# Four heads by 256 queries per attention unit, with the state-space and projection matmuls spread over the attention periods

## The chip, the cores and the metric

The kernel runs on one core of one Trainium2 chip. The metric is device microseconds (us) of one execution; lower is better.

The engines, as the profile names them: PE does matmuls and PEld is its weight load, which overlaps PE; ACT does the exponentials; DVE and POOL are two vector engines; SP issues most DMAs. "Granted clock" or PEclk is the share of full TensorE clock that the throttle granted. Two words for this kernel: PE writes its products to banks of PSUM (`ps` and `f_ps` in the views), and an "evacuation" is the copy that empties a bank into SBUF, where the other on-chip arrays lie.

## The reference, cut to what matters

```python
x = A_x                                                  # [1, 2048, 1024], bf16
g = sigmoid((x * gate_w).sum(-1, keepdims=True))
# a: diagonal complex state space model (SSM), 1024 states
Lam_bar = exp(dt * Lam);  B_bar = ((Lam_bar - 1) / Lam)[:, None] * Bmat
Bu = einsum("bld,pd->blp", x, B_bar)
for t in range(2048): h = Lam_bar * h + Bu[:, t]         # a scan over time
a = 2 * einsum("blp,dp->bld", hs, Cmat).real + x * Dskip
# b: attention, 32 heads of 32
q, k, v = x @ wqkv, split and transposed
b = softmax(q k^T * 32**-0.5) v, heads joined, @ wo
return g * a + (1 - g) * b
```

Attention needs 32 x 2048 x 2048 exponentials. Both kernels do them in 1024 ACT instructions of 128x1024 elements. The score array is held transposed (keys on the partitions), so that the exponentials can be the stationary operand ("weights") of the product with V (PV), which has only 33 columns: 32 of V and a column of ones for the softmax sum.

## The kernel before

Work is issued to the five engines in program order by a small scheduler that puts in the waits. The attention loop takes two heads and 512 queries per unit. Heads are 32 wide but Q and K are padded to 64 rows (POOL writes the masked copies), so the array is row-tiled two ways.

```python
def e_round(b):                       # one exp per round
    ...
    for h in range(2):                # L573: scores, two row tiles, 64 rows x 512 columns
        m = e.matmul(ps[:, 2*s+h, :], Ka[64*h:64*h+64, p%4, 128*kt:128*(kt+1)],
                     Qa[64*h:64*h+64, p%4, 512*qb:512*(qb+1)], ..., tile_position=(64*h, 0))
    S.op("act", lambda e: e.activation(pt[:, psl], ps[:, 2*s:2*s+2, :], ACT.Exp, scale=SCALE), ...)  # L577
    def pv(e):                        # L587: 8 pairs of weight load and 128x33 matmul
        for h in range(2):
            for qt in range(4):
                m = e.matmul(ps[:, 6, 33*gi:33*(gi+1)], pt[:, psl, h, 128*qt:128*(qt+1)], Va[...], ...)
```

The main loop fills PE between the exponentials with pieces of the next group's projections, two matmuls of 128x512 every second round, until they run out. Everything else of the SSM and the output projection comes after attention:

```python
while n < total_steps or pvq or misc or deferred:
    if n % 128 == 0: misc.extend(proj_pieces(g_next))    # last group: SSM input matmuls instead
    ...
    e_round(b)
    if n % 2 == 0: ...pop the PV tasks of earlier rounds...
    if n % 2 == 1 and misc: misc.pop(0)()                # dense filler, while there is any
    ...
    if n % 2 == 0 and bgp: bgp.pop(0)()                  # POOL: rotation tables, then fold of C
# after the loop: the rest of the SSM (u matmuls, scans, C matmuls) and the output projection
```

"Rotation tables" are built once per state block; they turn the complex scan into two real ones. "Folding C" multiplies the output matrix by complex constants, 96 elementwise operations of 128x512. Before, POOL does both during attention.

## Time and profile before

The median is 1334.15 us (2 runs, 1333.7 to 1334.61). The profiled execution spans 1338.0 us.

| stretch of the trace | us | what runs |
|---|---|---|
| to the first exp | 54.9 | loads, projection of all of group 0 |
| first to last exp | 1003.5 | attention with projections as filler |
| after the last exp | 279.6 | SSM and output projection, PE 93% busy (all the time from 1100 to 1300 us) |

These are lines of the profile page before: busy time and instructions of each engine; busy tenths in 40 equal slices of the span; the chain of waits that ended last, as shares of the span; and four of the costliest groups (line, engine, operation, output and input, count; then busy us, mean ns of one; then idle us of the engine just before them and what ended most of it).

```profile
PE 1225.9 (92%) x13313; PEld 592.2 (44%) x13313; DVE 346.0 (26%) x784; ACT 1039.1 (78%) x1218; POOL 330.6 (25%) x662
...
PE   4699989989998998999899989989988599999997
...
ACT  0399999999999999999999999999988522332211
...
PEclk8789969978995998699789959977998799999999
...
ACT 57%; PE 36%; DVE 3%; DMA 3%; issue 1%; SPq 0%; POOL 0%; POOLq 0%
...
L577 ACT ACTIVATE arena<-ps 128x1024 bf16<-128x1024 f32 x1024 | 952.7, 1039 | 32.9 <-PE ps L573 19.7
L587 PE MATMUL ps<-arena 128*128 128x33 bf16 x8192 | 373.6, 182 | 69.8 <-ACT arena L577 58.5
L573 PE MATMUL ps<-arena 64*128 64x512 bf16 x2048 | 424.1, 432 | 0.0
L587 PEld LDWEIGHTS ps<-arena 128*128 128x128 bf16 x8192 | 278.3, 98 | 288.6 <-ACT arena L577 151.2
```

PE is 92% busy over the whole span, but the chain is ACT for most of it and PE for the end: the kernel has two phases with two limits. In the last eight slices PE reads 9 (7 in the last) and ACT 1 to 3: a tail with no exponentials.

The windows view before, for the exps alone. The columns are the stretch, its length, ACT busy time in exps and their count, granted clock, DMA share, and GB/s.

```profile
80.00:170.00 90.00, 89.96 (x99) 0.99 0.02 5
170.00:192.00 22.00, 19.67 (x22) 0.50 0.01 1
192.00:285.00 93.00, 93.00 (x102) 1.00 0.17 38
285.00:312.00 27.00, 24.81 (x26) 0.50 0.00 1
```

While filler lasts, ACT is busy all the time and an exp comes every 0.92 us. Where it has run out (170 to 192 us, 285 to 312 us) the clock is granted at 0.50 and ACT has gaps. A window counts instructions that cross its edge in both neighbours, so counts are about one too high.

The timeline before, in a stretch with filler: start us, duration, then the instructions.

```profile
86.86 0.39 PE L573 MATMUL ps<-arena 64*128 64x512 bf16 x2
87.18 0.62 PEld L587 LDWEIGHTS ps<-arena 128*128 128x128 bf16 x16 [0.23 <-issue]
...
87.83 0.39 PE L573 MATMUL ps<-arena 64*128 64x512 bf16 x2
```

From the start of the scores to that of PV is 0.32 us, and from PV to the next scores 0.65 us. How that 0.65 divides into work and waiting becomes important below (the views merge the sixteen pairs into one line).

### The profile page before, as it was taken

To read this page: it belongs to the slowest core of one execution; us is meant where nothing else is said; L and a number is where in the kernel's file an instruction comes from. 1 tells how busy PE (TensorE), PEld (TensorE's weight loads), DVE (VectorE), ACT (ScalarE), POOL (GpSimd) and SP (SyncE) were. 2 spreads that over 40 slices of the span, in tenths; PEclk is the share of its full clock that TensorE was granted. 3 is DMA by queue.
4 is the path that set the end of the run, shared out by engine and by line. 5 is a ranking of instruction groups with operands and counts; after the bars stand their busy time and mean duration, and the time that the engine had idled before them with its cause. 6 is when DMAs were issued, how large, how long until landed. Compare 5 with 4: busy or idle time off the path is not lost.

```text
span 1338.0 us, 29670 instructions
## 1 busy us (share of the span) xinstructions
PE 1225.9 (92%) x13313; PEld 592.2 (44%) x13313; DVE 346.0 (26%) x784; ACT 1039.1 (78%) x1218; POOL 330.6 (25%) x662
## 2 busy tenths in 40 slices
PE   4699989989998998999899989989988599999997
PEld 1344634544463455345444534543433244444443
DVE  0211101100110110011001101100157668888840
ACT  0399999999999999999999999999988522332211
POOL 2213324322422341344557543100000000000000
PEclk8789969978995998699789959977998799999999
DMA  7220013003100400100010000000000031111011
GB/s 149 56 41 1 2 33 72 2 1 70 35 2 2 95 10 1 39 19 2 1 41 2 1 17 2 2 1 17 2 1 1 26 85 32 32 28 29 25 48 34
DMA packets 117353, 35.57 MB, mean 27 GB/s; under 512 B 114144, under 2 KB 114144, under 8 KB 117216
## 3 DMA queue, kind: packets, MB, share of 16 engines
q1 hardware_dynamic: 117216, 33.57, 11.1%
q8 instruction: 106, 1.74, 0.5%
q14 instruction: 31, 0.25, 0.1%
HBM read 8.40 MB, written 8.39 MB: 13 GB/s over the span
## 4 chain that ended last, share of the span: by engine, by line
ACT 57%; PE 36%; DVE 3%; DMA 3%; issue 1%; SPq 0%; POOL 0%; POOLq 0%
ACT arena L577 55%; PE ps L922 8%; PE ps L573 7%; PE ps L834 6%; PE ps L587 5%; PE ps L928 4%; PE ps L809 2%; PE ps L453 2%; DMA xT<-in_A_x_dram 2%; DVE arena L859 1%; DMA arena<-in_B_wo_dram 1%; PE ps L925 1%; PE ps L485 0%; DVE arena L399 0%; ACT L577 0%
## 5 line engine op out<-in xcount | busy, mean ns | idle before, releaser
L577 ACT ACTIVATE arena<-ps 128x1024 bf16<-128x1024 f32 x1024 | 952.7, 1039 | 32.9 <-PE ps L573 19.7
L587 PE MATMUL ps<-arena 128*128 128x33 bf16 x8192 | 373.6, 182 | 69.8 <-ACT arena L577 58.5
L573 PE MATMUL ps<-arena 64*128 64x512 bf16 x2048 | 424.1, 432 | 0.0
L587 PEld LDWEIGHTS ps<-arena 128*128 128x128 bf16 x8192 | 278.3, 98 | 288.6 <-ACT arena L577 151.2
L399 DVE CAST arena<-ps 128x512 bf16<-128x512 f32 x96 | 66.5, 693 | 508.7 <-PE ps L453 348.4
L453 PE MATMUL ps<-xT,arena 128*128 128x512 bf16 x512 | 165.5, 417 | 20.7 <-DMA arena<-in_B_wqkv_dram 10.2
L573 PEld LDWEIGHTS ps<-arena 64*128 64x128 bf16 x2048 | 91.2, 95 | 160.6 <-issue 130.5
L612 POOL TENSOR_TENSOR arena<-arena,gcol 128x8 f32<-128x8 f32 x64 | 13.0, 204 | 439.4 <-DVE arena L607 439.0
L922 PE MATMUL ps<-cT_re,arena 128*128 128x512 bf16 x256 | 98.0, 383 | 2.0 <-DMA arena<-out_dram 2.0
L922 PE MATMUL ps<-cT_im,arena 128*128 128x512 bf16 x256 | 98.0, 383 | 0.0
L607 DVE RECIPROCAL arena<-ps 128x8 f32<-128x8 f32 x64 | 13.3, 207 | 302.8 <-PE ps L587 302.8
L932 ACT ACTIVATE arena<-ps,gcol 128x512 bf16<-128x512 f32 x32 | 21.1, 679 | 79.7 <-PE ps L928 79.7
L485 PE MATMUL ps<-arena,xT 128*128 128x128 bf16 x1024 | 78.2, 221 | 3.2 <-DVE arena L399 3.2
L471 POOL TENSOR_SCALAR arena<-arena 128x512 bf16<-128x512 bf16 x64 | 48.7, 768 | 131.2 <-DVE arena L399 131.2
L859 DVE TENSOR_TENSOR_SCAN arena<-pf,init,arena 128x512 bf16<-128x512 f32 x64 | 78.5, 1269 | 0.0
L468 POOL TENSOR_SCALAR arena<-arena 128x512 bf16<-128x512 bf16 x64 | 43.7, 695 | 130.9 <-DVE arena L399 130.9
L453 PEld LDWEIGHTS ps<-xT,arena 128*128 128x128 bf16 x512 | 33.1, 101 | 91.0 <-issue 69.4
L485 PEld LDWEIGHTS ps<-arena,xT 128*128 128x128 bf16 x1024 | 57.8, 98 | 30.6 <-issue 26.0
L872 ACT ACTIVATE pf<-pf 128x1 f32<-128x1 f32 x24 | 7.1, 294 | 81.6 <-DVE pf L868 81.6
L838 ACT ACTIVATE arena<-ps 128x512 bf16<-128x512 f32 x48 | 27.6, 592 | 44.3 <-PE ps L834 44.3
L928 PE MATMUL ps<-arena 128*128 128x512 bf16 x256 | 60.5, 379 | 0.0
L834 PE MATMUL ps<-xT,bT_re 128*128 128x512 bf16 x192 | 47.0, 389 | 3.0 <-issue 3.0
(124 smaller groups left out, 738.9 us busy)
## 6 DMA issues: line engine op xcount, KB each, us to landing
arena<-in_B_wqkv_dram SPq DMA_DIRECT2D x24, 256.0 KB, 4.1
out_dram<-arena SPq DMA_DIRECT2D x8, 512.0 KB, 3.8
out_dram<-arena SPq DMA_DIRECT2D x16, 256.0 KB, 2.0
arena<-in_B_wo_dram SPq DMA_DIRECT2D x1, 2048.0 KB, 8.6
arena<-out_dram SPq DMA_TRANSPOSE x16, 3.1
bT_re<-in_A_B_re_dram SPq DMA_TRANSPOSE x8, 3.1
bT_im<-in_A_B_im_dram SPq DMA_TRANSPOSE x8, 3.1
cT_re<-in_A_C_re_dram SPq DMA_TRANSPOSE x8, 3.1
```

Source lines behind the costliest of these rows:

```text
L399: S.op("dve", lambda e: e.tensor_copy(dst, src), reads=r, writes=w, name=name)
L453: m = e.matmul(ps[:, 7, :], wring[:, g % 2, qk, dt_, :], xT[:, dt_, 512 * ch:512 * (ch + 1)], start=(dt_ == 0), stop=(dt_ == 7))
L468: pool(lambda e, dst=dst, mcol=mcol: e.tensor_scalar(dst, nat[:, 0, nb, :], mcol, 0.0, ALU.mult, ALU.add), [("nat", 0, nb), "msk"], [("qa" ...
L471: pool(lambda e, dst=dst, mcol=mcol, ocol=ocol: e.tensor_scalar(dst, nat[:, 1, nb, :], mcol, ocol, ALU.mult, ALU.add), [("nat", 1, nb), "m ...
L485: m = e.matmul(ps[:, 7, 128 * qtr:128 * (qtr + 1)], xT[:, dt_, 128 * kt:128 * (kt + 1)], wring[:, g % 2, 2, dt_, :], start=(dt_ == 0), sto ...
L573: m = e.matmul(ps[:, 2 * s + h, :], Ka[64 * h:64 * h + 64, p % 4, 128 * kt:128 * (kt + 1)], Qa[64 * h:64 * h + 64, p % 4, 512 * qb:512 * ( ...
L577: S.op("act", lambda e: e.activation(pt[:, psl], ps[:, 2 * s:2 * s + 2, :], ACT.Exp, scale=SCALE), reads=[("bank", 2 * s), ("bank", 2 * s ...
L587: m = e.matmul(ps[:, 6, 33 * gi:33 * (gi + 1)], pt[:, psl, h, 128 * qt:128 * (qt + 1)], Va[:, g % 2, kt, hh, :], start=(kt == 0 and h == 0 ...
L834: m = e.matmul(ps[:, 2 * st + ri, :], bT[ri][:, dt_, 128 * j:128 * (j + 1)], xT[:, dt_, 512 * ch:512 * (ch + 1)], start=(dt_ == 0), stop=( ...
L859: dve(lambda e, ri=ri: e.tensor_tensor_scan(ht[:, ri, :], rr, ut[:, ri, :], c.init[:, ri, j:j + 1], ALU.mult, ALU.add), [("ut", ri), ("ini ...
L922: m = e.matmul(ps[:, bank, :], hpv[ri][:, j, tcols], cT[ri][:, j, 512 * cb:512 * (cb + 1)], start=first, stop=last)
L928: m = e.matmul(ps[:, bank, :], OTt[:, osl, j, :], wo[:, j, 512 * cb:512 * (cb + 1)], start=first, stop=last)
```

## The change

The intent is one pipeline for everything. Each period issues one burst of scores for four heads and 256 queries (four row tiles of 32 rows, no padding), two exps, PV of an earlier burst, and four 128x512 matmuls of "dense" work from one list: projections, gate, SSM, output projection. SSM evacuations and rotation tables are on DVE; all dense chains share one PSUM bank. The input x is loaded in smaller pieces and transposing DMAs are no longer serialized against the others. The old code stays as a fallback that a range check on the softmax sums would start.

The diff rewrites the fast path, so only its core is shown; long argument lists are cut with "...".

```diff
@@ scheduler: transposing DMAs are serialized only on request
-    def __init__(self, n_dma_lanes=12, pool_in_order=False):
+    def __init__(self, n_dma_lanes=12, pool_in_order=False, serial_xpose=False):
...
-        if dma:
+        if dma and self.serial_xpose:
@@ the attention burst (new class)
+    def burst(self, B):
+        ...
+            for kl in range(2):
+                for h in range(4):              # L1413
+                    m = e.matmul(ps[:, 2*sl[h//2]+h%2, 256*kl:256*(kl+1)],
+                                 K[32*h:32*h+32, g%2, 128*kt:128*(kt+1)],
+                                 Q[32*h:32*h+32, qz, qo:qo+256], ..., tile_position=(32*h, 0))
+        for z in range(2):                      # L1419
+            self.act(lambda e, s=s, p=p: e.activation(pt[:, p], ps[:, 2*s:2*s+2, :], ACT.Exp, scale=SCALE), ...)
@@ a dense chain: matmuls into bank 7, then one evacuation on DVE
+    def d_u(self, j, ch, n, ri):
+        ...                                     # 8 matmuls of 128x512, L1318
+        def evac():
+            self.dve(lambda e: e.tensor_copy(self.ub[:, n%2, ri, :], ps[:, 7, :]), ...)     # L1322
+            if ri == 1:
+                if ch == 0:
+                    self.bg += self.table_ops(j)       # 22 DVE operations: a rotation table
+                self.bg += self.item_ops(j, ch, n)     # 14 or 15 DVE operations: rotate, scan, rotate
@@ folding C, still on POOL
+    def pool_fold(self):
+        for j in range(8):
+            self.ld_c(j)
+            for hf in range(2):                 # 6 POOL operations of 128x512, 96 in all
+                pool(... X, ci, a2 ...); pool(... Y, cr, a2 ...); pool(... Z, cr, a1 ...)
+                pool(... cr = Z + X ...); pool(... Z, ci, b2 ...); pool(... ci = Y + Z ...)
@@ the loop over 512 periods
+        for p in range(NBURST + 2):
+            self.burst(p)
+            if p >= 2: self.pv(p - 2)
+            if p == 12 and not folded:
+                self.pool_fold()
+            quota = MM_PER_PERIOD if start == [] else 8      # 4, and 8 while group 0 is projected
+            while used < quota: ...issue dense pieces, chains chosen by a static rule...
+            while self.bg: ...issue DVE side jobs while a modelled DVE time allows...
+            if ended is not None: ended.evac()
```

The static rule orders DVE's work with a model of its time: a table operation of n columns is taken as 0.08 + n/960 us.

## The prediction

> **What bounds the kernel now.** The table of windows splits the 1338 us profile in three. (1) 0 to 55 us: loading and projecting the first group; in the timeline the first exp starts at 54.9 us (x lands in four serialized steps of about 6 us). (2) 55 to 1060 us: attention, 1024 exps of 128x1024; the chain of waits gives ACT 57%. Where dense projection work fills PE, the clock is 1.00 and exps start every 0.918 us (11 exps in 10.21 us). Where a group's projections have run out, PE is still about 80% busy, but the granted clock is 0.50 and exps come every 1.04 us. The seven long ACT pieces of the chain hold 702 exps in 644 us; the other 322 take 361 us, 1.12 us each: about 65 us lost. (3) 1060 to 1338 us: SSM and out-projection, PE 100% busy at 216 ns per 128x512 matmul. Those 278 us are pure PE.
>
> **What the change does.** It moves the dense work of (3) into (2): four matmuls per period of two exps. QK goes from two row tiles (twice 0.32 us per two exps) to four row tiles and 256 queries: array time halves. The throttled stretches lose their cause: I count dense work in about 440 of the 448 periods before the last group, which out-projection fills. SSM evacuations move from ACT to DVE (about 500 us of 940 by estimate: hidden, but one PSUM bank serves all dense chains).
>
> **Cost of a period.** ACT floor: 2 x 0.917 = 1.834 us, times 512 = 939 us. PE, from the timeline: 16 PV pairs 0.54 us (34 ns each); dense 4 x 0.216 = 0.864; drain before the tile mode changes 0.11; QK: 2 x 0.107 array + 0.107 mode change = 0.32 at best. The Trainium skill, "TensorE: Matmul & The Clock Gate", "Measured speedup vs the span model", has four row tiles of K=32 at 3.07x, not 4x; no run here shows it yet; I estimate 0.34 to 0.40. Sum 1.85 to 1.91 us: PE becomes the bound by a little. Three score slots serve two per burst, so PE can be late by only some 0.15 us before ACT stalls; the 17-piece C chains add a fifth dense piece 32 times, up to 7 us. Attention: 512 x 1.87 = 957, plus about 5.
>
> **Ends.** Start: x in smaller pieces, not serialized, weights on the second queue: first exp at about 14 us; the first eight periods carry eight dense pieces and wait for x: +10. Tail: PV, normalize, transposing DMA (3.1 us), one matmul, add, store: about 9 us. Total 14 + 10 + 962 + 9 = 995: about 278 gained at the tail, 40 at the start, 65 from the clock; 10 given back at the tail, about 30 to a longer period.
>
> **What shows it.** Granted clock over 0.97 throughout; exp pitch 0.92 to 0.95 us; QK start to PV start 0.34 to 0.40; PE the largest share in the chain of waits; first exp before 18 us; no PE-only tail.
>
> **What would make it wrong.** QK at 0.5 us (weight loads not overlapping): 1040. Clock dropping in spite of the dense work (the skill's same page, "The HAM clock gate", halves it after an idle window; here it fell at 80% busy): up to 1080. DVE late for the single bank, PE waiting on evacuations: +20 to 50. PE at its best and ACT bound: 965.

## The result, and the profile after

The median is 1027.85 us (2 runs, 1027.32 to 1028.38), faster by a ratio of 0.7704 with a 95% interval of 0.7671 to 0.7737. A ratio is the mean time of one kernel's fast runs over that of the other's of the same rounds, so it is not quite the ratio of the quoted medians. The profiled execution spans 1026.6 us.

| stretch of the trace | before, us | after, us | gained |
|---|---|---|---|
| to the first exp | 54.9 | 19.5 | 35.4 |
| first to last exp | 1003.5 | 993.3 | 10.2 |
| after the last exp | 279.6 | 13.8 | 265.8 |
| span | 1338.0 | 1026.6 | 311.4 |

So attention takes 10 us less although it now contains nearly all the work of the old tail (266 us shorter). These are the lines of the page after that answer to those before.

```profile
PE 915.7 (89%) x15153; PEld 489.6 (48%) x15375; DVE 522.9 (51%) x1118; ACT 948.1 (92%) x1034; POOL 106.8 (10%) x142
...
PE   5976768898999999999999999999999999799995
...
DVE  3259998988788533451126761137775112122223
ACT  3775559999999999999999999999999999999994
POOL 1089990000000000000000000000000000000000
PEclk9978789999999999999999999999999999899998
...
ACT 75%; DVE 12%; PE 9%; SPq 3%; issue 1%; DMA 1%
...
L1419 ACT ACTIVATE f_pt<-f_ps 128x1024 bf16<-128x1024 f32 x1024 | 942.7, 1234 | 50.6 <-PE f_ps L1413 50.6
L1435 PE MATMUL f_ps<-f_V,f_pt 128*128 128x33 bf16 x8192 | 292.1, 179 | 3.9 <-DVE f_On L1449 3.5
L1413 PE MATMUL f_ps<-f_Q,f_K 32*128 32x256 bf16 x4096 | 207.4, 277 | 26.6 <-ACT f_pt L1419 8.8
```

ACT is now 92% busy and 75% of the chain. Its slices read 9 almost from end to end, except slices 2 to 6 (about 26 to 154 us), where they read 7, 7, 5, 5, 5. In the last four of these POOL reads 8, 9, 9, 9, DVE 5, 9, 9, 9, and the clock drops to 7 and 8. The chain has 12% DVE. The windows view after, for the exps, columns as before, says how much is lost where:

```profile
19.00:60.00 41.00, 31.09 (x34) 0.92 0.74 124
60.00:110.00 50.00, 31.84 (x34) 0.83 0.57 93
110.00:160.00 50.00, 31.16 (x33) 0.80 0.18 25
...
262.00:890.00 628.00, 628.00 (x686) 1.00 0.20 48
```

From 262 to 890 us ACT has no gap: one piece of the chain of waits holds 693 exps in 635.43 us, 0.917 us each. 1024 exps at that pace take 939 us; attention took 993, so 54 us are gaps. By the windows (counts less one, times 0.917) about 10 of these are before 60 us, 40 between 60 and 160 us, and the rest is scattered. The waits view of 60 to 200 us names who held ACT and who held PE: total us, times, longest (`f_OT` holds the scratch of the rotation tables).

```profile
ACT f_pt L1419 <- PE f_ps L1413: 39.2, 19, 10.2
...
PE f_ps L1318 <- DVE f_OT L1190: 13.7, 2, 9.9
...
PE f_ps L1318 <- DVE f_ub L1322: 6.5, 2, 5.3
```

ACT waits 39 us for scores (L1413), with one wait of 10 us. PE, which would write those scores, is in front of the next dense chain (L1318) and waits for DVE to empty the one dense bank. Where the view names a table operation as what ended the wait, an evacuation had ended just before: in the longest wait, 9.9 us, the evacuation L1322 ends at 80.45 us, PE goes on at 80.97, and the operation named lies between. This is one instance in the timeline after; brackets give idle time before and its releaser.

```profile
111.20 0.67 DVE L1322 CAST f_ub<-f_ps 128x512 bf16<-128x512 f32 x1
...
112.39 1.49 PE L1318 MATMUL f_ps<-f_xT,f_wb 128*128 128x512 bf16 x3 [5.29 <-DVE f_ub L1322]
...
113.81 0.61 PE L1413 MATMUL f_ps<-f_Q,f_K 32*128 32x256 bf16 x8
...
114.48 1.94 ACT L1419 ACTIVATE f_pt<-f_ps 128x1024 bf16<-128x1024 f32 x2 [5.96 <-PE f_ps L1413]
```

The evacuation at 111.20 us comes late because DVE works in order and has table and rotation operations ahead of it. PE waits 5.29 us, and as PE is in order too, the scores behind wait with it, and ACT idles 5.96 us.

The steady period, from the timeline after at 500 us:

```profile
500.91 0.40 PE L1413 MATMUL f_ps<-f_Q,f_K 32*128 32x256 bf16 x8
501.23 0.46 PEld L1435 LDWEIGHTS f_ps<-f_V,f_pt 128*128 128x128 bf16 x16 [0.21 <-issue]
...
501.65 1.02 PE L1269 MATMUL f_ps<-f_xT,f_wb 128*128 128x512 bf16 x4
...
502.74 0.12 PEld L1413 LDWEIGHTS f_ps<-f_Q,f_K 32*128 32x128 bf16 x8 [0.56 <-ACT f_pt L1419]
```

Scores to PV take 0.32 us; 16 PV pairs to the dense work 0.40 us; and before the next scores PE waits for ACT to free a score slot. In the steady state ACT is the limit, not PE.

### The profile page after: what moved, and what is told of

It is laid out like the page before. It is cut to its first block, busy times and chain, and to the rows that moved or that the text cites. A ratio compares the mean times of both kernels' runs of the same rounds, so it can differ in the third digit from the quotient of the medians.

```text
span 1026.6 us, 33366 instructions
## 1 busy us (share of the span) xinstructions
PE 915.7 (89%) x15153; PEld 489.6 (48%) x15375; DVE 522.9 (51%) x1118; ACT 948.1 (92%) x1034; POOL 106.8 (10%) x142
## 4 chain that ended last, share of the span: by engine, by line
ACT 75%; DVE 12%; PE 9%; SPq 3%; issue 1%; DMA 1%
ACT f_pt L1419 75%; SPq L1007 2%; PE f_ps L1435 2%; PE f_ps L1269 2%; PE f_ps L1318 2%; PE f_ps L1413 2%; DVE f_OT L1189 2%; DVE f_OT L1193 2%; DVE f_tq L1209 2%; DVE f_OT L1191 2%; PE f_ps L1287 1%; DVE f_OT L1190 1%; DVE f_ut L1209 1%; DVE f_ub L1322 1%; SPq L1016 1%
## 5 line engine op out<-in xcount | busy, mean ns | idle before, releaser
L1419 ACT ACTIVATE f_pt<-f_ps 128x1024 bf16<-128x1024 f32 x1024 | 942.7, 1234 | 50.6 <-PE f_ps L1413 50.6
L1435 PE MATMUL f_ps<-f_V,f_pt 128*128 128x33 bf16 x8192 | 292.1, 179 | 3.9 <-DVE f_On L1449 3.5
L1435 PEld LDWEIGHTS f_ps<-f_V,f_pt 128*128 128x128 bf16 x8192 | 239.6, 96 | 115.6 <-issue 108.3
L1413 PE MATMUL f_ps<-f_Q,f_K 32*128 32x256 bf16 x4096 | 207.4, 277 | 26.6 <-ACT f_pt L1419 8.8
L1413 PEld LDWEIGHTS f_ps<-f_Q,f_K 32*128 32x128 bf16 x4096 | 61.1, 92 | 245.2 <-ACT f_pt L1419 230.3
L1318 PE MATMUL f_ps<-f_xT,f_wb 128*128 128x512 bf16 x448 | 124.6, 396 | 37.1 <-DVE f_OT L1190 13.7
L1269 PE MATMUL f_ps<-f_xT,f_wb 128*128 128x512 bf16 x450 | 119.4, 385 | 16.8 <-DMA f_xT<-in_A_x_dram 6.1
L1218 DVE TENSOR_TENSOR_SCAN f_ht<-f_pf,f_init,f_ut 128x512 bf16<-128x512 f32 x64 | 81.4, 1296 | 0.0
L1344 PE MATMUL f_ps<-f_cT_im,f_hp 128*128 128x512 bf16 x192 | 72.6, 378 | 6.0 <-DVE f_Ag L1359 4.1
L1322 DVE CAST f_ub<-f_ps 128x512 bf16<-128x512 f32 x64 | 44.2, 690 | 55.8 <-PE f_ps L1318 55.7
L1318 PEld LDWEIGHTS f_ps<-f_xT,f_wb 128*128 128x128 bf16 x512 | 41.7, 98 | 62.0 <-issue 31.8
L1287 PE MATMUL f_ps<-f_wb,f_xT 128*128 128x128 bf16 x1024 | 67.9, 220 | 3.0 <-DVE f_K L1276 1.7
L1269 PEld LDWEIGHTS f_ps<-f_xT,f_wb 128*128 128x128 bf16 x512 | 41.2, 97 | 45.5 <-issue 11.7
```

What stands on the lines that cost most here:

```text
L1218: ops.append((1.25, lambda ri=ri: dve(lambda e: e.tensor_tensor_scan(ht[:, ri, :], rr, ut[:, ri, :], self.init[:, ri, j:j + 1], ALU.mult, ...
L1269: mms.append((1, lambda e, f, l, a=a: e.matmul(ps[:, bank, :], w[:, g % 2, part, a, :], xT[:, a, 512 * ch:512 * (ch + 1)], start=f, stop=l ...
L1287: m = e.matmul(ps[:, bank, 128 * q:128 * (q + 1)], xT[:, a, 128 * kt:128 * (kt + 1)], w[:, g % 2, 2, a, :], start=(a == 0), stop=(a == 7))
L1318: mms.append((1, lambda e, f, l, a=a: e.matmul(ps[:, 7, :], bT[:, n % 2, ri, a, :], xT[:, a, 512 * ch:512 * (ch + 1)], start=f, stop=l), [ ...
L1322: self.dve(lambda e: e.tensor_copy(self.ub[:, n % 2, ri, :], ps[:, 7, :]), [("bank", 7)], [("ub", n % 2, ri)], "evac_u")
L1344: mms.append((1, lambda e, f, l, j=j, ri=ri: e.matmul(ps[:, 7, :], hp[:, ri, j, cols], cT[ri][:, j, 512 * cb:512 * (cb + 1)], start=f, sto ...
```

## The experiments

Theory A: the 40 us at 60 to 160 us come from POOL folding C at the same time as DVE builds tables, each making the other slower through their common SBUF port, so that DVE is late for the single bank. Rival B: DVE simply has too much to do there (tables), with or without POOL. Rival C: the start (serialized or split loads) shifts everything. For the steady state: theory P is the prediction's (PE is the bound), theory Q says PE has slack. Three batches ran, each on one chip; the kernel before took 1335.92, 1335.93 and 1337.35 us (medians) in them. The change was not run again in these batches. The medians of the kernel before, with 1334.15 in the first measurement, differ by up to 3 us, so a difference to the change of less than that is not resolved.

| run | what it changes | median us | ratio to before |
|---|---|---|---|
| the change | | 1027.85 | 0.7704 |
| x1_no_fold | POOL's fold left out (wrong result) | 992.57 | 0.7438 |
| x2_one_table | one table in place of eight | 1006.81 | 0.7538 |
| e4_before_filler | the kernel before, with dummy matmuls | 1306.24 | 0.9777 |
| x5_more_pv | 8 more PV pairs per period | 1069.90 | 0.8016 |
| x3_fold_dve | fold on DVE | 1000.96 | 0.7491 |
| x8_fold_early | POOL's fold ten periods earlier | 1022.70 | 0.7657 |
| x7_serial | transposing DMAs serialized again | 1027.98 | 0.7704 |
| x10_x0_whole | first quarter of x in one load | 1028.24 | 0.7697 |
| x11_combined | x3 and a rearranged start | 1004.90 | 0.7524 |
| x12_qk_twice | every score matmul twice | 1080.52 | 0.8091 |

### x1_no_fold: take the fold away

The C chains use the matrix unfolded, so the result is wrong on purpose (relative error 0.119). The loads stay.

```diff
         for j in range(8):
             self.ld_c(j)
-            ...the 12 POOL operations per j...
@@ C chains
-                            [("hp", b, j, ri), ("cTf", ri, j, cb)]))
+                            [("hp", b, j, ri), ("cT", ri, j)]))
```

> The changed kernel without the 96 POOL operations that fold the B scale into C (the result is wrong on purpose; every other instruction and the static order stay). Theory A, POOL's reads of SBUF hold up DVE between 55 and 157 us, DVE is late for the one dense bank, PE waits in order behind it and ACT runs dry: DVE operations there go back to their later durations (a 128x16 scalar_tensor_tensor at about 0.25 us instead of 0.6 to 1.3), most of the 40 us lost between 60 and 200 us come back, 990 to 1000 us. Rival B, DVE simply has too much work of its own there (rotation tables and items): less than 10 us come back, over 1018 us.

Measured: 992.57 us (990.98 to 995.84), 35 us less than the change. DVE was given the same operations. The windows of x1 for the exps:

```profile
60.00:110.00 50.00, 48.94 (x54) 1.00 0.68 105
110.00:160.00 50.00, 48.73 (x54) 1.00 0.18 37
```

54 exps in place of 34, and the clock is 1.00. The groups view by shape shows why. This is DVE of the change between 60 and 150 us: count, busy us and mean ns.

```profile
L1209 DVE TENSOR_TENSOR f_tq<-f_ub,f_Et 128x512 bf16<-128x512 bf16 x12 | 8.2, 721 | 0.1
...
L1322 DVE CAST f_ub<-f_ps 128x512 bf16<-128x512 f32 x8 | 5.5, 683 | 3.2 <-PE f_ps L1318 3.1
L1209 DVE TENSOR_TENSOR f_ut<-f_tq 128x512 f32<-128x512 bf16 x4 | 5.1, 1320 | 0.0
...
L1191 DVE SCALAR_TENSOR_TENSOR f_OT<-f_OT,f_W 128x16 f32<-128x16 f32 x3 | 2.1, 707 | 0.0
```

And the same operations in x1 (its lines are 14 lower):

```profile
L1308 DVE CAST f_ub<-f_ps 128x512 bf16<-128x512 f32 x11 | 7.6, 688 | 4.3 <-PE f_ps L1304 4.3
L1195 DVE TENSOR_TENSOR f_tq<-f_ub,f_Et 128x512 bf16<-128x512 bf16 x17 | 6.5, 420 | 0.2
...
L1195 DVE TENSOR_TENSOR f_ut<-f_tq 128x512 f32<-128x512 bf16 x8 | 5.1, 684 | 0.0
...
L1177 DVE SCALAR_TENSOR_TENSOR f_OT<-f_OT,f_W 128x16 f32<-128x16 f32 x5 | 1.1, 229 | 0.0
```

A product with two SBUF inputs takes 721 ns beside POOL and 420 without; a sum 1320 and 684; a table operation of 16 columns 707 and 229. The evacuation, whose one input is in PSUM, takes 683 and 688: untouched. This is what the Trainium skill states in "SBUF — State Buffer", section "Who interferes with whom": a DVE instruction with two SBUF inputs, or in a two-port mode, contends with the other vector engine for a shared port pair, which is locked and not split (for a whole instruction, it says of the two-port modes), and one with at most one SBUF input outside these modes does not. The trace agrees on both sides. POOL is slowed too: its fold operations take means of 0.77 to 1.34 us in the same stretch of the change, and 0.70 and 1.27 us in the kernel before. Short operations suffer most in proportion, which fits a lock held for a whole POOL operation, though not all do: another table operation of 16 columns (L1190, three executions) took 229 ns beside POOL and 228 without. The runs show which operations slow down beside POOL; that a lock is the reason rests on the page. Theory A is confirmed as to the overlap, and taking the fold away is worth 35 us.

### x2_one_table: take most tables away

```diff
-            ops.append((c, lambda: dve(fn, r, w)))
+            ops.append((c, (lambda: dve(fn, r, w)) if j == 0 else (lambda: None)))
@@ the rotations use table 0 throughout
-        er, ei = self.Et[:, 0, j, :], self.Et[:, 1, j, :]
+        er, ei = self.Et[:, 0, 0, :], self.Et[:, 1, 0, :]
```

> The changed kernel with the rotation table of tile 0 used for all eight tiles (wrong on purpose), so that 154 DVE operations of table building drop out while POOL's fold and the static order stay. Theory A (POOL holds DVE up): the items and evacuations left are still slowed, only a part comes back, 1000 to 1012 us. Rival B (too much work on DVE): nearly all comes back, 985 to 995 us. Both could be partly true: then x1 and x2 each give about half.

Measured: 1006.81 us (1005.1 to 1007.53), 21 us less than the change. The window from 60 to 110 us still has only 38 exps; that from 110 to 160 us has 51. The kernel was meant to be wrong, but its result passed the tolerance, so passing it says little about the tables. Fewer DVE operations help, as both theories say, but less than removing POOL does, with all tables in place. Rival B alone fails: in x1 DVE had every table to build and was on time.

### e4_before_filler: the clock, in the kernel before

Two dummy matmuls go into the free bank in every second round, once the projections have run out. This measures what dense work is worth through the clock, less whatever the dummy matmuls cost.

```diff
+    def filler(e):
+        for _ in range(2):
+            m = e.matmul(ps[:, 7, :], xT[:, 0, 0:128], xT[:, 0, 0:512], start=True, stop=True)
@@ main loop
             if misc:
                 misc.pop(0)()
+            elif fast and n < 16 * NU:
+                S.op("pe", filler, reads=[xtoks[0]], writes=[("bank", 7)], name="filler")
```

> The kernel before with two dummy 128x512 matmuls into the free dense bank wherever a group's projections have run out. Theory of the prediction, the halved clock in these stretches costs about 65 us: clock 1.00 through the attention, exps every 0.918 us there too, 1265 to 1285 us, although PE does more work. Rival, the stretches are slow for another reason and the low clock is only a sign of it: within 10 us of 1334, or slower.

Measured: 1306.24 us (1304.51 to 1308.34), ratio 0.9777 with interval 0.9747 to 0.9807: a gain of 30 us, and the expectation of twice that missed. (The record's verdict is "unclear", as the interval straddles a gain of 2%; that there is a gain is clear, as the interval lies below 1.) The windows of e4 for the exps:

```profile
80.00:872.00 792.00, 792.00 (x865) 1.00 0.09 20
872.00:1030.00 158.00, 135.61 (x147) 0.93 0.02 5
```

Up to 872 us ACT has no gap left and the clock is 1.00, with 865 exps where the kernel before has 837 at a clock of 0.89: more matmuls made the kernel faster. The last stretch did not improve (1.07 us per exp before, 1.08 here); it holds the last group, where SSM steps run on ACT and DVE between the exps. So of the 65 us that the prediction put down to the clock, about 30 come back with the clock; the rest lies mostly in the start of attention and the last group.

### x5_more_pv: how much slack PE has

```diff
-                    for h2 in range(2):
+                    for h2 in (0, 0, 1):
```

Eight more pairs of weight load and matmul per period (start flags kept right; the products of two of the four heads are added twice, in numerator and denominator alike, so the result stays right).

> The changed kernel with the PV matmuls of two of four heads done twice (the numerator and denominator of these heads both double, so the result stays right): eight more 33-column pairs, about 0.20 us more PE work in each of 512 periods. If PE now needs 1.70 us of a period of 1.834 (read from the trace after: QK 0.32, PV 0.41, dense 0.86, mode change 0.11), the first 0.13 us are free: 1050 to 1070 us. If PE is the bound, as the prediction had it, all of it shows: +100 us, about 1130 us.

Measured: 1069.90 us (1068.34 to 1071.78), 42 us more than the change. From 250 to 890 us, 666 exps took 640 us: 1.92 us per period where the change has 1.834.

```profile
250.00:890.00 640.00, 634.36 (x666) 1.00 0.20 45
```

Eight pairs at the change's pace, (0.46 - 0.096) / 15 = 0.024 us each, are 0.20 us. So PE without them needs about 1.72 us, and has some 0.11 us of slack. If PE had been the bound, the whole 0.20 us, about 100 us over 512 periods, would have shown. Theory Q holds.

### x12_qk_twice: what four row tiles are worth

```diff
-            for kl in range(2):
+            for kl in (0, 1, 0, 1):
```

> The changed kernel with every score matmul issued twice (same values, right result), so that QK takes as much array time per period as with two row tiles. From x5: a full period of PE work is about 1.72 us without additions, so 0.21 us more gives 1.93 us against 1.834: 1068 to 1085 us. If the repeated matmuls overlap the mode change and cost less: 1030 to 1060 us. If PE had no slack: over 1120 us.

Measured: 1080.52 us (1078.98 to 1083.19), 53 us more. In the timeline at 501.46 us the 16 matmuls take 0.54 us to the start of PV, where 8 take 0.32.

```profile
501.46 0.62 PE L1413 MATMUL f_ps<-f_Q,f_K 32*128 32x256 bf16 x16
502.00 0.47 PEld L1435 LDWEIGHTS f_ps<-f_V,f_pt 128*128 128x128 bf16 x16 [0.21 <-issue]
```

With 0.54 us of scores per period PE is the bound. The run keeps four row tiles and only doubles their work, so it stands in for two row tiles; by it, the rest of the change would not fit under the exps without the narrower tiles.

### x3_fold_dve: fold on DVE, which is faster at it

The fold moves to DVE as 64 scalings and 32 sums, all bf16. C is loaded in period 1 and folded from period 7 on. DVE's later work comes later, so the last C chains run at six matmuls per period. The result is right.

```diff
-                pool(...six operations...)                # per j and half
+            ts(0, ci, a2, ...); ts(1, cr, a2, ...); ts(2, cr, a1, ...); ts(3, ci, b2, ...)   # DVE
+            tt(cr, 2, 0, ...); tt(ci, 1, 3, ...)
@@ the loop
-            if p == 12 and not folded:
+            if p == 1:
                 self.pool_fold()                           # now diagonal of Dskip and loads only
+            if 7 <= p < 15:
+                self.bg += self.fold_ops(p - 7)
-            quota = MM_PER_PERIOD if start == [] else 8
+            quota = 8 if start else 6 if g == 6 and not us and p >= 424 and (...C chains left...) else MM_PER_PERIOD
```

> The changed kernel with the fold done right, but on DVE (64 bf16 products and 32 bf16 sums, about 24 us by the durations of the trace) in the periods from 7 on, C loaded from period 1 on, and the last C chains at six matmuls per period, because the static order would not fit otherwise. POOL does nothing in attention but the carries. If holding up by POOL is the cause and not the fold's own work: DVE operations at their quiet durations, 994 to 1006 us, right result. If the added 24 us of DVE work cost as much as POOL's contention did: 1015 us or more.

Measured: 1000.96 us (999.87 to 1002.13), ratio 0.7491 with interval 0.7467 to 0.7515: 27 us faster than the change and the fastest kernel here with a right result. The windows of x3 for the exps:

```profile
60.00:110.00 50.00, 48.29 (x53) 1.00 0.24 48
110.00:160.00 50.00, 48.57 (x54) 0.93 0.18 39
```

DVE got 36 us more work (64 at 0.347 and 32 at 0.417 us), and the exps came on time. DVE's operations are at their quiet durations (products 419 ns). This tells theory A from rival B most plainly: the cost is not in how much DVE does, but in POOL's work beside it.

### x8_fold_early: the same overlap, sooner

```diff
-            if p == 12 and not folded:
+            if p == 2 and not folded:
```

> The changed kernel with C loaded and folded on POOL from period 2 on instead of period 12 (one number changed), so that some 20 of POOL's 100 us fall where DVE is nearly idle. Theory A: the loss is set by the overlap of POOL's and DVE's work, a fifth to a third of it goes: 1010 to 1022 us. Rival: the place of the fold does not matter, 1028 us, or the earlier C loads delay the first groups and it gets slower, over 1030 us.

Measured: 1022.70 us (1022.26 to 1023.3), 5 us less, just outside the expected range: an eighth of the 40 us and not a fifth to a third. It is a gain all the same: x7 and x10, of the same batch and as slow as the change, have no run under 1025.9. From 60 to 160 us there are 35 and 38 exps in place of 34 and 33. POOL works about as long (103.7 us in place of 106.8), only sooner; moving the overlap recovers a little, removing it recovers 35 us.

### x7_serial and x10_x0_whole: what holds the first exp

```diff
@@ x7_serial
-        S = Sched(n_dma_lanes=14)
+        S = Sched(n_dma_lanes=14, serial_xpose=True)
@@ x10_x0_whole
-        for q in range(4):
-            self.ld_x(128 * q, 128 * (q + 1), ("x0", q))
+        self.dma(lambda e: e.dma_start_transpose(self.xT[:, :, 0:512], self.x2[0:512, :]), [], [("x0", q) for q in range(4)], "ld_x")
```

> The changed kernel with the old rule that a transposing load waits for every other load and the others for it. The prediction put the gain at the start on this: first exp 5 to 10 us later, the third and fourth quarter of x some 10 us later, and the loads of B and the transposes of attention output wait for each other all along: 1040 to 1060 us. If the order of loads costs nothing after the first: within 10 us of 1028.

> The changed kernel with the first 512 rows of x loaded by one transposing load, as before the change, instead of four of 128 rows, each of which takes 1.3 us or more to issue. In the trace after, the first projection waits for x until 12.2 us. If the four issues are what delays it: projection starts at 8 to 10 us, first exp 2 us or more before 19.5, 1024 to 1027 us. If ACT's and DVE's chain of parameter arithmetic holds the first exp: it stays at 19 us or later, 1027 to 1029 us.

Measured: 1027.98 us (1025.9 to 1031.29) and 1028.24 us (1027.64 to 1028.77), both the same as the change. x7 misses the 1040 to 1060 us of its first theory. Serializing the transposing DMAs again costs nothing, and the first exp is at 19.1 us. But the rule hardly moved the loads: the last transposing load of x is issued at 20.1 us, in the change at 19.2. One load for the first quarter of x starts the projection at 10.4 us in place of 12.2, but the first exp is still at 20.3 us (19.8 to 20.3 in x1, x2 and x3, whose start is that of the change). What holds it is elsewhere: in the timeline of the change ACT issues weight and parameter loads until 12.57 us and then does parameter arithmetic, with three table loads of 1.28 us, until 19.45 us, while DVE's share of that arithmetic (until 17.8 us) stands before the evacuation of Q and K. That the gain of 35 us at the start comes from needing only one chunk each of K and Q before the first exp is thus likely, but argued from the code: no run has the new start without it, and the two old ways of loading were put back singly, not together. Rival C fails: neither run changes the total.

### x11_combined: x3 with a start rearranged after that finding

One load for the first quarter of x, weights first on ACT's queue, parameters on SP's, and the parameter arithmetic after the third burst.

```diff
-        self.math(pw2, iot)
+        self.math_in = (pw2, iot)
@@ the loop
+            if p == 3:
+                self.math(*self.math_in)
+                self.bg += self.math2()
```

> x3 (fold on DVE) with a leaner start: one load for the first 512 rows of x, the three weight loads first on ACT's queue, the five parameter loads behind x on SP's, and the parameter arithmetic after the third burst instead of before the first. If ACT's DMA issues (to 13 us) and the arithmetic behind them hold the first exp at 19.5 us, as x10 hints: first exp at 13 to 16 us, and 3 to 6 us less than x3, 995 to 998 us. If the start is bound by the arrival of x and by the eight dense pieces per period, the earlier first exp only waits more often later: 999 to 1002 us.

Measured: 1004.90 us (1004.08 to 1005.7), ratio 0.7524 (0.7507 to 0.7542): a miss, 4 us slower than x3 in another batch, where the intervals just overlap; in any case no gain. The first exp did come at 16.93 us. But this is in the timeline of x11:

```profile
33.18 0.61 PE L1416 MATMUL f_ps<-f_Q,f_K 32*128 32x256 bf16 x8 [5.40 <-DVE f_K L1278]
```

PE waits 5.40 us for an evacuation of K that stands behind the parameter arithmetic on DVE; that arithmetic takes DVE from 25.66 to 32.44 us, with 0.91 us of waiting for a parameter load, which now comes later. The stall was moved, not removed, and grew: up to 60 us ACT did 28.4 us of exps, in x3 30.5.

## Why the prediction was right or wrong

The time came close: 1027.85 against 995, 3% over. The sum behind it, against the trace:

| term | predicted | measured | difference |
|---|---|---|---|
| first exp | 14 | 19.5 | +5.5 |
| start-up periods with eight dense pieces | 10 | about 10 | 0 |
| 1024 exps at the steady pace | 957 | 939 | -18 |
| other gaps in attention | 5 | about 44 | +39 |
| after the last exp | 9 | 13.8 | +5 |
| sum | 995 | 1026.6 | +32 |

The second row agrees in size only. The prediction had PE wait for x there; from 19 to 60 us PE does not, and its longest named wait is 2.4 us in all, for DVE's evacuations of K.

**Folding the tail in: right.** The tail went from 279.6 to 13.8 us, and the four matmuls per period cost no ACT time in the steady state. That is the change's main gain. (The old tail was not quite "pure PE": PE was 93% busy in it.)

**"PE becomes the bound by a little": wrong.** The step that failed is the cost of a period, 1.85 to 1.91 us. It took 0.54 us for 16 PV pairs out of a timeline in which the second eight wait for the next exp: the page before charges 151 us of idle before these weight loads to ACT. In the burst at 87.18 us of the timeline above, the single records of the trace put the weight loads 15 to 29 ns apart, except the ninth: it starts 183 ns after the eighth, just after an exp ends at 87.48 us. Without the wait, as in the change, where PV takes exps of two bursts earlier, they take 0.40 us, a pair every 24 ns. The Trainium skill, "TensorE: Matmul & The Clock Gate", section "Wait — 56ns, not 53.3ns?", gives about 25 ns as the floor between the starts of small matmuls, and the trace agrees. Scores took 0.32 us, the best case. So PE needs about 1.72 us (x5) against ACT's 1.834, and the bound is ACT. The step's mechanism, a sum of PE's work, was right; its PV term was 0.14 us too large and its scores 0.02 to 0.08. The text had this branch as its "PE at its best": 965.

**DVE "hidden": wrong, and this cost more than the period gained.** The text named the risk (DVE late for the single bank, +20 to 50) but called the evacuations hidden, as it set DVE's total work against the whole span. The 40 us were lost within one stretch of 100 us. The cause, POOL's fold slowing DVE, was not in the prediction at all. The fold is in the kernel before too, where DVE had little to do and the overlap cost nothing: in e4 it runs from 602 to 783 us, where ACT has no gap. x1 gives 35 us for it; x3 recovers 27 with a right result.

**"65 from the clock": right that it was lost, half wrong in its cause.** The low-clock stretches of the kernel before went, but e4 puts only about 30 us down to the clock. The granted clock stayed at 1.00 from 262 to 890 us, as predicted, but not "over 0.97 throughout": it was 0.80 to 0.83 at 60 to 160 us, where PE waited, 0.69 at 890 to 910 us, and 0.964 overall.

**The start: size wrong and reason wrong.** The first exp is at 19.5 us, not "before 18", and putting the serializing rule back changed nothing (x7). The queue of loads on ACT and the parameter arithmetic hold it (x10): with both moved, it comes at 16.93 us (x11), though the total does not gain.

**The chain:** PE was to have the largest share. It is ACT's, 75%, as ACT is the bound.

Two errors of opposite sign, -18 and +39, partly cancel in the sum: that the total came so close is in part luck. Of the six things that the prediction named for checking, only the last, no PE-only tail, came out as written; clock, exp pitch (0.917 us in the steady state, 0.97 over attention), QK start to PV start (0.32), chain and first exp did not.

What stays open: how the 40 us divide between PE standing still and PE running slower, since the granted clock is lower there too (0.80 to 0.83, and 1.00 in x1); and the 10 us before 60 us, of which only the first-exp part was tried.

## What to carry to other kernels

When an engine goes from idle to busy, look again at the jobs that overlap it: the fold on POOL was free while DVE idled (e4), and cost 35 of 1028 us once DVE had work, in a stretch where one late evacuation stops PE and then ACT, because queues are in order and there is one bank. To cost a step from a trace, take it from a place where its group has no wait inside; the gap between two groups' starts is an upper bound. And check a total's terms singly: here two wrong ones partly cancelled.

## What the Trainium skill lacked or had wrong

- "SBUF — State Buffer", "Who interferes with whom": agrees as far as it goes; for size it has only two ratios, DVE 6.8 times and the other engine 1.5 times slower, without shapes. Here DVE products went from 420 to 721 ns, sums from 684 to 1320, and operations of 16 columns from 229 to 707.
- "ScalarE: Activation LUTs", "What ACT_TABLE_LOAD costs": 186 ns + 0.833 ns per element less an overlap of 93 ns is 0.946 us per exp of 1024 columns, by an estimate from its figures. The trace has 0.917 us (693 exps in 635.43 us). In the kernel before, one exp takes 1039 ns on average, as the first two figures give, so it is the overlap that is larger here, about 122 ns. Its table load of 1283 ns agrees (1.28 us).
- "TensorE: Matmul & The Clock Gate", "Measured speedup vs the span model": 3.07 for four row tiles of K=32, N=512. Doubling the scores (x12) added 0.22 us for 8 matmuls of 32x256; one after another they would take 8 x 0.108 = 0.86 us, estimated from 0.216 us per 128x512. That is 3.9 times, for the second half of a burst. The whole single burst, with its change of tile mode, takes 0.32 us, 2.7 times.
- The same page, Part 1 "The HAM clock gate", ties the half clock to an idle window, and "A second HAM failure mode" to short idles between groups, where it has the clock go to and fro. In the kernel before it stayed at 0.50 for 22 us with PE 87% busy in the windows view (19.08 of 22 us, matmul ends being modelled), and dummy matmuls (e4) brought it back to 1.00 (from 80 to 872 us). How busy PE must be to keep its clock is not on the page, and no run here settles it.
